# Mask triangles of the first layer moved to GpSimd, and small TensorE work in column strips

## The chip, the cores and the metric

The kernel runs on one core of a Trainium2 chip. The metric is device time in microseconds (us) from the first to the last instruction. Before the change the median of three runs is 2272.32 us (2268.7 to 2274.12). The profile is one execution of 2267.0 us.

A core has five engines with queues of their own that run in order: TensorE (PE, and PEld for its weight loads), VectorE (DVE), ScalarE (ACT), GpSimd (POOL) and SyncE (SP). They wait for each other through semaphores. GpSimd and SyncE also issue DMA transfers, in the order in which they stand in their queues.

## The reference: what is computed

Four attention layers follow one another, each of the form x + attention(layernorm(x)) on x of 2048 rows and 640 columns in bfloat16. Layers 0 and 2 (A) use a causal window of 256 keys; layers 1 and 3 (B) see all keys. All have 32 heads of 20 columns.

```python
mask = (idx[:, None] - idx[None, :] >= 0) & (idx[:, None] - idx[None, :] < W)   # W = 256, layers A
scores = jnp.where(mask[None, None], scores, -1e9)
p = _softmax(scores, axis=-1)
o = jnp.einsum("bhqk,bhkd->bhqd", p, v)
return (lambda x, *d: x.transpose(*d))(o, 0, 2, 1, 3).reshape(B, S, D) @ wo
...
x = x + _A_ref(_layernorm(x, axis=-1), A_wqkv, A_wo)
x = x + _B_ref(_layernorm(x, axis=-1), B_wqkv, B_wo)
```

The pair of lines at the end is run twice with the same weights.

## The kernel before

Work is cut into units: one layer, one chunk of 512 queries (four chunks, c), one group of four heads (eight groups, g). Layer 3's and layer 1's first chunks are cut further by keys. Within a unit the work goes by banks. A bank is a PSUM bank of 128 keys by 512 columns for one head: scores are computed with the keys on the partitions, so the probabilities can go straight into the product with the values. Two or three banks make a tile; the tiles alternate between two halves of the scores' PSUM.

For each tile the kernel emits, in this order: the score matmuls (line 1305, four heads in four row strips of the array), one exponential on ScalarE from PSUM to a bfloat16 tile pt in SBUF (line 1336), then side work, then the products of probabilities and values of a group of banks two or three tiles back (P·V, line 1369, in column strips of 21 columns), and last the masks of the tile before. In the windowed layers P·V trails by three tiles.

The values carry a column of ones, so row 20 of each head's strip in the output holds the sum of the probabilities. When a unit ends, VectorE copies the output to SBUF (line 856), and a tail (t_tail) is queued for every two units: it picks the row sums by small matmuls with a selector of four columns (line 1042), takes reciprocals on VectorE (line 1047), splits them into two bfloat16 halves, transposes them (line 1059), spreads them over the heads' rows by matmuls (line 1080) and multiplies (line 1084).

Side work is a list of Python generators (LayerNorm, projections, values, output projection, tails). A planner written into the kernel keeps a credit per tile and a due unit for each task, and so fixes the order of all instructions when the program is built. It also keeps an account of TensorE's activity and fills quiet places with matmuls whose result nobody reads (unread)[...]. Projections and fillers use by_columns (line 297): one product as four matmuls of 32 output columns each, in four column strips of the array. Weights of the projections are loaded by DMA from GpSimd's queue (line 334), and projected keys and queries are written to DRAM from the same queue (line 530).

LayerNorm's task (t_ln) scales 128 rows on VectorE (line 414), transposes them in five full 128 x 128 pieces on TensorE (line 432) and copies them out (line 320, on ScalarE or VectorE).

Masks. A windowed unit of a later chunk has three kinds of bank per head, m = 0, 1, 2, each with two key blocks laid into 512 columns. In blocks of 128 columns, m = 0 has triangles in blocks 0, 1 and 3, m = 1 in blocks 1 and 2, and m = 2 in blocks 0, 2 and 3: eight for each head. The unmasked blocks are full. In layer 0, line 1406 sets the two triangles of m = 1 with GpSimd's affine_select, in place on pt. Line 1416 multiplies all 512 columns (from the first block in use) of m = 0 and m = 2 by a bfloat16 mask on VectorE, one instruction for neighbouring banks of one m in a tile. Layer 2 does all masks on VectorE. In the first chunk the banks hold fewer blocks.

Layer 0 and the first part of layer 1 are woven: from the last group of layer 0's second chunk on, units of both alternate. Up to there, ScalarE copies the projections out of PSUM, after it VectorE does.

Of the kernel before, what the change touches and what calls it, by code (L numbers as in the profile page):

```python
# [12 lines left out]
ALU = mybir.AluOpType  # L13
ACT = mybir.ActivationFunctionType

P = 128
# [7 lines left out]
C = 512  # L24
# [22 lines left out]
def kernel(  # L47
# [10 lines left out]
    nc = tc.nc  # L58
# [33 lines left out]
    ident = big.tile([P, P], BF16, name="ident", tag="ident")  # L92
    nhalf = big.tile([P, 4], F32, name="nhalf", tag="nhalf")
    sel4 = big.tile([P, 4], BF16, name="sel4", tag="sel4")
    spread4 = big.tile([64, 4, P], BF16, name="spread4", tag="spread4")
    masks = big.tile([P, 3, C], BF16, name="masks", tag="masks")
# [8 lines left out]
    op = ps[:, 7, :]  # L105
# [10 lines left out]
    for h in range(2):  # L116
        for n in range(2):
            a = n * D + h * HD
# [10 lines left out]
    def load_wop(w, dense):  # L129
# [9 lines left out]
        out=ident[:], in_=ident[:], compare_op=ALU.not_equal, fill=1.0,  # L139
        base=0, pattern=[[-1, P]], channel_multiplier=1,  # L140
# [5 lines left out]
    for m, b, ge in (  # L146
# [4 lines left out]
        v = masks[:, m, b * P : (b + 1) * P]  # L151
        nc.gpsimd.affine_select(
            out=v, in_=v, compare_op=ALU.is_ge if ge else ALU.is_gt, fill=0.0,
            base=0, pattern=[[1 if ge else -1, P]], channel_multiplier=-1 if ge else 1,
# [138 lines left out]
    def by_columns(out_, lhsT, rhs, start, stop):  # L293

        for j in range(4):
            r = slice(32 * j, 32 * j + 32)
            nc.tensor.matmul(out_[r], lhsT=lhsT[:, r], rhs=rhs, start=start, stop=stop)  # L297
# [92 lines left out]
    def t_ln(l, c):  # L390
        while ("x", l, c) not in ready:
            yield ("wait", 1)
        yield from room("xnT", "ln")
        for n in (1, 0):
            order = worder[l, n]
            if order and not any(e in wtiles for e in order):
                wtiles[order[0]] = get_w(*order[0])
        users[l, c] = 9 if (l, c) == (0, 0) else (11, 12, 11, 11)[l]
        mv = mvs.pop((l, c))
        rstd = lnp.tile([P, 4], F32, name="rstd", tag="rstd")  # L400
        nc.gpsimd.tensor_scalar(  # L401
            out=rstd[:], in0=mv[:, :, 1], scalar1=EPS, scalar2=1.0, op0=ALU.add, op1=ALU.mult
        )
        nc.gpsimd.tensor_tensor(out=rstd[:], in0=rstd[:], in1=nhalf[:], op=ALU.pow)
        yield ("wait", 2)
        nmr = lnp.tile([P, 4], F32, name="nmr", tag="nmr")
        nc.vector.scalar_tensor_tensor(
            out=nmr[:], in0=mv[:, :, 0], scalar=-1.0, in1=rstd[:], op0=ALU.mult, op1=ALU.mult
        )
        xt = xtp.tile([P, KD, C], BF16, name="xnT", tag="xnT")  # L410

        def normed(i):
            xn = xnp.tile([P, D], BF16, name="xn", tag="xn")
            nc.vector.tensor_scalar(
                out=xn[:], in0=x_sb[:, 4 * c + i, :],
                scalar1=rstd[:, i : i + 1], scalar2=nmr[:, i : i + 1],
                op0=ALU.mult, op1=ALU.add,
            )
            return xn

        rows = deque([normed(0)])
        yield ("wait", 1)
        for i in range(4):
            if i < 3:
                rows.append(normed(i + 1))
            xn = rows.popleft()
            mb = yield from take_m()
            for _ in range(1+(l<2)):
                unread(mb)
            trp = ps[:, mb, :].bitcast(BF16)[:, 0 : KD * P].rearrange("p (c m) -> p c m", c=KD)  # L430
            for dc in range(KD):
                nc.tensor.transpose(  # L432
                    out=trp[:, dc, :], in_=xn[:, dc * P : (dc + 1) * P], identity=ident[:]
                )
            evac(xt[:, :, i * P : (i + 1) * P], trp)
            drop_m(mb)
            yield ("pe", 0.4)
        xnT[l, c] = xt
        live["ln"] -= 1
        ready.add(("xnT", l, c))  # L440
# [192 lines left out]
    def unread(b):  # L633

        by_columns(ps[:, b, :], ident, masks[:, 0, :], True, True)
        state["heat"] += 1.0
# [386 lines left out]
    def t_tail(us):  # L1023
        final = us[-1][0:3] == (3, NC - 1, G - 1)

        def fill(count):

            for n in range(count * final):
                nc.tensor.matmul(
                    ps[:, 0, :], lhsT=ident[:], rhs=masks[:, 0, :], start=True, stop=True  # L1030
                )

        n = len(us)
        yield ("wait", 2)
        fill(2)
        mb = yield from take_m()
        warm_bank(mb)
        zp = ps[:, mb, 0 : 16 * n]
        for i, (l, c, g, oT) in enumerate(us):
            for qb in range(4):  # L1040
                a = 16 * i + 4 * qb
                nc.tensor.matmul(  # L1042
                    zp[:, a : a + 4], lhsT=oT[:, qb * P : (qb + 1) * P],
                    rhs=sel4[:], start=True, stop=True,
                )
        rz = rzp.tile([P, 2, 16], F32, name="rz", tag="rz")[:, 0:n, :]
        nc.vector.reciprocal(out=rz.rearrange("p u r -> p (u r)"), in_=zp)
        drop_m(mb)

        hl = rzp.tile([P, 2, 2, 16], BF16, name="hl", tag="hl")[:, 0:n]  # L1050
        nc.vector.tensor_copy(out=hl[:, :, 0, :], in_=rz)
        nc.vector.tensor_tensor(out=hl[:, :, 1, :], in0=rz, in1=hl[:, :, 0, :], op=ALU.subtract)
        yield ("pe", 0.25)
        fill(3)
        yield ("wait", 2)
        mb = yield from take_m()
        warm_bank(mb)
        rp = ps[0 : 32 * n, mb, :].bitcast(BF16)[:, 0:P]
        nc.tensor.transpose(
            out=rp, in_=hl.rearrange("p u n r -> p (u n r)"), identity=ident[:]  # L1060
        )
        rT = rzp.tile([64, P], BF16, name="rT", tag="rT")
        nc.vector.tensor_copy(out=rT[0 : 32 * n], in_=rp)
        drop_m(mb)
        yield ("pe", 0.1)
        fill(1)
        yield ("wait", 2 if state["tick"] < last_tick[0] else 1)
        for i in range(n):
            yield from scaled(*us[i], 32 * i, rT, fill)
        if any(packed(l, c) for l, c, g, oT in us):  # L1070
            yield ("wait", 2)
        for u in us:
            yield from settle(*u)
# [121 lines left out]
    with tc.manual_schedule():  # L1195
# [14 lines left out]
        n = 0  # L1210
        last_layer = sum(len(u.banks) for u in units[: index[3, 1, 0, None]])
        placed = {}
        while n < last_layer:
            size = 2 if len(tiles) % 2 and narrow(banks[n][0]) else 3
            u = banks[n][0]
# [52 lines left out]
        while ended is None or t < ended + 8:  # L1268
# [3 lines left out]
            if t < len(tiles) or banks:  # L1272
# [9 lines left out]
                for b in cur:  # L1282
                    u = b[0]
# [18 lines left out]
                for n in range(2):  # L1302
                    for i, (u, j, m, b0, subs, first, last, end) in enumerate(cur):
                        for kc, q0, qn, col in subs[n : n + 1]:
                            nc.tensor.matmul(  # L1305
                                sp[:, i, col * P : (col + qn) * P],
                                lhsT=u.k(kc, j), rhs=u.q(j, q0, qn), start=True, stop=True,
# [22 lines left out]
                i = 0  # L1330
                while i < n_b:
                    b0 = cur[i][3]
                    k = i
                    while k < n_b and cur[k][3] == b0:
                        k += 1
                    nc.scalar.activation(  # L1336
                        out=pt[:, i:k, b0 * P :], in_=sp[:, i:k, b0 * P :],
                        func=ACT.Exp, scale=SCALE,
                    )
                    i = k  # L1340
# [5 lines left out]
                r = rate(t)  # L1346
# [6 lines left out]
            for n in range(2 if n_b == 0 or t > closed + 1 else 0):  # L1353
                u = pts[0][3][0] if pts else None
# [11 lines left out]
                for m, (kc, q0, qn, col) in enumerate(subs):  # L1366
                    for _, pg, i, b in group:
                        j = b[1]
                        nc.tensor.matmul(  # L1369
                            op[32 * j : 32 * j + VW, q0 * P : (q0 + qn) * P],  # L1370
                            lhsT=u.v(kc, j), rhs=pg[:, i, col * P : (col + qn) * P],
                            start=(first and m == 0), stop=(last and m == len(subs) - 1),
                            skip_group_check=u.windowed,
                        )
                if end and u.aside:
                    pair = side_done(u)
                    for n, j in enumerate(u.aside):
                        nc.tensor.matmul(  # L1378
                            op[32 * j : 32 * j + VW, :], lhsT=u.v(NT - 1, j),
                            rhs=pair[n // 2][:, n % 2, :], start=False, stop=True,  # L1380
# [12 lines left out]
            if t > 0 and masked is not None:  # L1393
                cur_, pt_ = masked
                i = 0
                while i < len(cur_):
                    m, b0 = cur_[i][2:4]
                    k = i
                    while k < len(cur_) and cur_[k][2] == m:
                        k += 1  # L1400
                    if m == 1 and cur_[0][0].l == 0:
                        for b in (1, 2):
                            if b < b0:
                                continue
                            v = pt_[:, i:k, b * P : (b + 1) * P]
                            nc.gpsimd.affine_select(  # L1406
                                out=v, in_=v, compare_op=ALU.is_gt if b == 1 else ALU.is_ge, fill=0.0,
                                base=0, pattern=[[0, k - i], [-1 if b == 1 else 1, P]],
                                channel_multiplier=1 if b == 1 else -1,
                            )  # L1410
                    elif m is not None:
                        cols = slice(max(b0, m == 1) * P, 3 * P if m == 1 else C)
                        mv_ = masks[:, m, cols].unsqueeze(1).to_broadcast(
                            (P, k - i, cols.stop - cols.start)
                        )
                        nc.vector.tensor_tensor(  # L1416
                            out=pt_[:, i:k, cols], in0=pt_[:, i:k, cols], in1=mv_, op=ALU.mult
                        )
                    i = k
# [36 lines left out]
```

The softmax here doesn't subtract the row's maximum and nothing guards it: scores larger than these inputs give would overflow.

## Time and profile before

| What | Value |
|---|---|
| median of three runs | 2272.32 us |
| lowest, highest | 2268.7, 2274.12 us |
| profiled execution, first to last instruction | 2267.0 us |
| ScalarE busy | 2166.5 us (96%) |
| TensorE busy, by its modelled ends | 1973.3 us (87%) |
| VectorE busy | 1269.8 us (56%) |
| GpSimd busy | 326.2 us (14%) |
| GpSimd's selects, line 1406 | 126, 55.8 us, between 21 and 383 us |
| VectorE's mask multiplies, line 1416 | 331, 191.0 us, of which 136 and 86.0 us between 20 and 385 us |
| full-array transposes, line 432 | 300 matmuls, 28.4 us |
| row sums, line 1042 | 512 matmuls, 22.7 us |
| transposes of reciprocals, line 1059 | 65 matmuls, 15.8 us |

A busy time is the union of an engine's instructions. A group's row gives the line, the engine, the operation, what is written and read with its shape, the number of instructions, the busy time, the mean length of one in ns, and the idle time of the engine just before them with what ended it. A shape such as 128*32 128x512 of a matmul means 128 rows and 32 columns of the array, moving 512 columns; 32*128 is a row strip and 128*32 a column strip. The chain of work is followed back from the last instruction, at each step to what released it.

### The profile page before, as it was taken

How to read it: one execution, taken by the hardware profiler on the slowest of the kernel's cores; microseconds unless marked ns; L12 is line 12 of the kernel's file. 1: busy time of each engine (PE TensorE's matmuls, PEld its weight loads, DVE VectorE, ACT ScalarE, POOL GpSimd, SP SyncE). 2: the span in 40 equal slices, each digit the busy share in tenths (PEclk: the TensorE clock that was granted, in tenths of full speed). 3: DMA queues.
4: the chain of work that ended last, by engine and by line, in shares of the span. 5: the costliest groups of instructions: out<-in, count | busy, mean ns of one | idle time of the engine just before them, and what ended most of it. 6: DMA issues, size and time to landing. Idle time of an engine off the chain costs nothing.

```text
span 2267.0 us, 65801 instructions
## 1 busy us (share of the span) xinstructions
PE 1973.3 (87%) x28523; PEld 776.0 (34%) x28524; DVE 1269.8 (56%) x2158; ACT 2166.5 (96%) x1740; POOL 326.2 (14%) x571
## 2 busy tenths in 40 slices
PE   8999998988888888888888988898888888888887
PEld 3444343334333333333333443342322222222222
DVE  6766575435554565555564644442566666656665
ACT  7789899999999989999899999999999999999998
POOL 4454334201100122001210022002000000000000
PEclk9999999999999999999999999999999999999999
DMA  6233223422210233002330033103211111111100
GB/s 195 72 91 94 74 87 93 100 76 50 78 34 15 60 88 104 17 28 58 93 90 15 16 106 105 31 17 91 65 51 31 31 40 34 31 31 43 42 21 16
DMA packets 88384, 136.80 MB, mean 60 GB/s; under 512 B 20766, under 2 KB 63486, under 8 KB 88094
## 3 DMA queue, kind: packets, MB, share of 16 engines
q1 hardware_dynamic: 68878, 79.43, 12.6%
q0 software_dynamic: 19216, 53.17, 8.0%
q8 instruction: 223, 3.65, 0.7%
q14 instruction: 67, 0.55, 0.1%
HBM read 99.52 MB, written 27.79 MB: 56 GB/s over the span
## 4 chain that ended last, share of the span: by engine, by line
ACT 49%; PE 23%; issue 17%; DVE 9%; POOL 1%; DMA 1%; SPq 0%; ACTq 0%; DVEq 0%; POOLq 0%
ACT pt L1336 47%; PE ps L297 14%; PE ps L1305 5%; PE ps L1369 2%; DVE pt L1416 1%; ACT ka L1336 1%; DVE x_sb L562 1%; DVE st L320 1%; DVE on L1084 1%; PE ps L432 1%; PE ps L1080 0%; DVE vs L320 0%; DVE va L320 0%; PE ps L1042 0%; DVE raw_o L909 0%
## 5 line engine op out<-in xcount | busy, mean ns | idle before, releaser
L1336 ACT ACTIVATE pt<-ps 128x1536 bf16<-128x1536 f32 (+2 forms) x1636 | 2089.3, 1462 | 64.8 <-PE ps L1305 56.2
L297 PE MATMUL ps<-masks,ident 128*32 128x512 bf16 x6452 | 553.2, 388 | 113.2 <-ACT pt L1336 59.1
L1305 PE MATMUL ps<-qt,kt 32*128 32x512 bf16 x4004 | 545.7, 384 | 85.5 <-ACT pt L1336 77.6
L1369 PE MATMUL ps<-pt,vt 128*21 128x512 bf16 x3844 | 392.2, 382 | 0.1
L1305 PEld LDWEIGHTS <-kt 32*128 32x128 bf16 x4004 | 163.4, 91 | 544.1 <-issue 526.8
L297 PEld LDWEIGHTS <-ident 128*32 128x32 bf16 x6452 | 162.0, 94 | 361.6 <-issue 350.4
L1416 DVE TENSOR_TENSOR pt<-pt,masks 128x1024 bf16<-128x1024 bf16 (+6 forms) x331 | 191.0, 604 | 154.9 <-ACT pt L1336 154.1
L297 PE MATMUL ps<-xnT,wqk 128*32 128x512 bf16 x3320 | 221.7, 385 | 17.1 <-DVE st L320 7.9
L320 DVE CAST st<-ps 128x512 bf16<-128x512 f32 x134 | 92.6, 691 | 188.1 <-PE ps L297 187.7
L909 DVE TENSOR_SCALAR xnT<-ps 128x512 int32<-128x512 f32 x92 | 63.6, 691 | 191.4 <-PE ps L902 191.3
L297 PE MATMUL ps<-wop,on 128*32 128x320 bf16 x3712 | 156.9, 301 | 13.3 <-DVE x_sb L562 8.4
L1305 PE MATMUL ps<-qa,ka 32*128 32x384 bf16 (+2 forms) x1408 | 117.9, 276 | 32.0 <-ACT pt L1336 29.4
L1369 PEld LDWEIGHTS <-vt 128*21 128x21 bf16 x3956 | 102.5, 91 | 110.4 <-issue 64.8
L1084 DVE TENSOR_TENSOR on<-on,ps 128x512 bf16<-128x512 bf16 x128 | 86.3, 683 | 67.0 <-PE ps L1080 65.3
L297 PE MATMUL ps<-wv,xnT 128*32 128x320 bf16 x2560 | 112.4, 301 | 10.8 <-DVE on L1084 3.3
L297 PEld LDWEIGHTS <-wqk 128*32 128x32 bf16 x3320 | 79.1, 96 | 112.8 <-issue 59.4
L562 DVE TENSOR_TENSOR x_sb<-x_sb,ps 128x320 bf16<-128x320 bf16 x120 | 58.0, 483 | 104.9 <-PE ps L297 104.7
L297 PEld LDWEIGHTS <-on 128*32 128x32 bf16 x3712 | 92.8, 96 | 65.9 <-issue 49.2
L856 DVE CAST on<-ps 128x512 bf16<-128x512 f32 x112 | 77.0, 687 | 59.9 <-PE ps L1378 32.9
L401 POOL TENSOR_SCALAR rstd<-mv 128x4 f32<-128x4 f32 x15 | 3.8, 253 | 712.4 <-DVE mv L388 702.8
L1305 PEld LDWEIGHTS <-ka 32*128 32x128 bf16 x1408 | 43.2, 92 | 117.0 <-issue 110.9
L1369 PE MATMUL ps<-pt,va 128*21 128x384 bf16 (+2 forms) x1408 | 76.9, 281 | 4.6 <-POOL pt L1406 3.5
(100 smaller groups left out, 1589.8 us busy)
## 6 DMA issues: line engine op xcount, KB each, us to landing
vt<-v_d SPq DMA_DIRECT2D x48, 336.0 KB
kt<-k_d SPq DMA_DIRECT2D x192, 80.0 KB
wqk<-in_B_wqkv_dram POOLq DMA_DIRECT2D x80, 160.0 KB, 3.6
wqk<-in_A_wqkv_dram POOLq DMA_DIRECT2D x70, 160.0 KB, 3.3
k_d<-st POOLq DMA_DIRECT2D x75, 128.0 KB, 2.2
q_d<-st POOLq DMA_DIRECT2D x75, 128.0 KB, 2.2
qt<-q_d SPq DMA_DIRECT2D x384, 20.0 KB
v_d<-vs POOLq DMA_DIRECT2D x16, 336.0 KB, 3.4
```

The costliest lines, as they stand in the source:

```text
L297: nc.tensor.matmul(out_[r], lhsT=lhsT[:, r], rhs=rhs, start=start, stop=stop)
L320: nc.vector.tensor_copy(out=out_, in_=in_)
L401: nc.gpsimd.tensor_scalar(out=rstd[:], in0=mv[:, :, 1], scalar1=EPS, scalar2=1.0, op0=ALU.add, op1=ALU.mult)
L432: nc.tensor.transpose(out=trp[:, dc, :], in_=xn[:, dc * P : (dc + 1) * P], identity=ident[:])
L562: nc.vector.tensor_tensor(out=xv, in0=had, in1=yp, op=ALU.add)
L856: nc.vector.tensor_copy(out=oT, in_=op)
L909: V.tensor_scalar(out=xi.bitcast(I32)[:, i * C : (i + 1) * C], in0=side["psum"], scalar1=SCALE * LOG2E * E23, scalar2=-128.0 * E23, op0=AL ...
L1084: nc.vector.tensor_tensor(out=oT, in0=oT, in1=zb, op=ALU.mult)
L1305: nc.tensor.matmul(sp[:, i, col * P : (col + qn) * P], lhsT=u.k(kc, j), rhs=u.q(j, q0, qn), start=True, stop=True,)
L1336: nc.scalar.activation(out=pt[:, i:k, b0 * P :], in_=sp[:, i:k, b0 * P :], func=ACT.Exp, scale=SCALE,)
L1369: nc.tensor.matmul(op[32 * j : 32 * j + VW, q0 * P : (q0 + qn) * P], lhsT=u.v(kc, j), rhs=pg[:, i, col * P : (col + qn) * P], start=(first ...
L1416: nc.vector.tensor_tensor(out=pt_[:, i:k, cols], in0=pt_[:, i:k, cols], in1=mv_, op=ALU.mult)
```

## The change

The masks of layer 0 are split differently. GpSimd now also sets the triangle in block 3 of m = 0 and that in block 0 of m = 2, so it has four of the eight. VectorE multiplies only columns 0 to 255 of m = 0 and columns 256 to 511 of m = 2, where the other two triangles of each bank lie. Each such group of banks has one instruction on either engine where there was one on VectorE. Layer 2 stays as it was. The aim is to relieve VectorE in the first layer.

The transposes of LayerNorm, the row sums and the transposes of the reciprocals are emitted in column strips of 32 columns, as the projections already are: 20 matmuls in place of 5, 32 in place of 8 for two units, and two in place of one. The aim is to keep TensorE in one tile shape. The planner's accounts are not touched, so the order of the tasks stays the same.

```diff
--- before.py
+++ after.py
@@ -429,9 +429,12 @@
                 unread(mb)
             trp = ps[:, mb, :].bitcast(BF16)[:, 0 : KD * P].rearrange("p (c m) -> p c m", c=KD)
             for dc in range(KD):
-                nc.tensor.transpose(
-                    out=trp[:, dc, :], in_=xn[:, dc * P : (dc + 1) * P], identity=ident[:]
-                )
+                for j in range(4):
+                    a = dc * P + 32 * j
+                    nc.tensor.transpose(
+                        out=trp[32 * j : 32 * j + 32, dc, :], in_=xn[:, a : a + 32],
+                        identity=ident[:],
+                    )
             evac(xt[:, :, i * P : (i + 1) * P], trp)
             drop_m(mb)
             yield ("pe", 0.4)
@@ -1039,10 +1042,7 @@
         for i, (l, c, g, oT) in enumerate(us):
             for qb in range(4):
                 a = 16 * i + 4 * qb
-                nc.tensor.matmul(
-                    zp[:, a : a + 4], lhsT=oT[:, qb * P : (qb + 1) * P],
-                    rhs=sel4[:], start=True, stop=True,
-                )
+                by_columns(zp[:, a : a + 4], oT[:, qb * P : (qb + 1) * P], sel4[:], True, True)
         rz = rzp.tile([P, 2, 16], F32, name="rz", tag="rz")[:, 0:n, :]
         nc.vector.reciprocal(out=rz.rearrange("p u r -> p (u r)"), in_=zp)
         drop_m(mb)
@@ -1056,9 +1056,11 @@
         mb = yield from take_m()
         warm_bank(mb)
         rp = ps[0 : 32 * n, mb, :].bitcast(BF16)[:, 0:P]
-        nc.tensor.transpose(
-            out=rp, in_=hl.rearrange("p u n r -> p (u n r)"), identity=ident[:]
-        )
+        for i in range(n):
+            nc.tensor.transpose(
+                out=rp[32 * i : 32 * i + 32], in_=hl[:, i].rearrange("p n r -> p (n r)"),
+                identity=ident[:],
+            )
         rT = rzp.tile([64, P], BF16, name="rT", tag="rT")
         nc.vector.tensor_copy(out=rT[0 : 32 * n], in_=rp)
         drop_m(mb)
@@ -1398,17 +1400,26 @@
                     k = i
                     while k < len(cur_) and cur_[k][2] == m:
                         k += 1
-                    if m == 1 and cur_[0][0].l == 0:
-                        for b in (1, 2):
-                            if b < b0:
-                                continue
-                            v = pt_[:, i:k, b * P : (b + 1) * P]
-                            nc.gpsimd.affine_select(
-                                out=v, in_=v, compare_op=ALU.is_gt if b == 1 else ALU.is_ge, fill=0.0,
-                                base=0, pattern=[[0, k - i], [-1 if b == 1 else 1, P]],
-                                channel_multiplier=1 if b == 1 else -1,
-                            )
-                    elif m is not None:
+                    split = m is not None and cur_[0][0].l == 0
+                    for b in ((3,), (1, 2), (0,))[m] if split else ():
+                        if b < b0:
+                            continue
+                        later = (m, b) in ((1, 1), (0, 3))
+                        v = pt_[:, i:k, b * P : (b + 1) * P]
+                        nc.gpsimd.affine_select(
+                            out=v, in_=v, compare_op=ALU.is_gt if later else ALU.is_ge, fill=0.0,
+                            base=0, pattern=[[0, k - i], [-1 if later else 1, P]],
+                            channel_multiplier=1 if later else -1,
+                        )
+                    if split and m != 1:
+                        cols = slice(max(b0, 0) * P, 2 * P) if m == 0 else slice(2 * P, C)
+                        mv_ = masks[:, m, cols].unsqueeze(1).to_broadcast(
+                            (P, k - i, cols.stop - cols.start)
+                        )
+                        nc.vector.tensor_tensor(
+                            out=pt_[:, i:k, cols], in0=pt_[:, i:k, cols], in1=mv_, op=ALU.mult
+                        )
+                    elif m is not None and not split:
                         cols = slice(max(b0, m == 1) * P, 3 * P if m == 1 else C)
                         mv_ = masks[:, m, cols].unsqueeze(1).to_broadcast(
                             (P, k - i, cols.stop - cols.start)
```

## The prediction

> **What bounds the kernel now.** First the whole-span busy line of the page (PE 87%, ACT 96%, DVE 56%, POOL 14%), which averages over unlike stages. Then busy time by stretch, cut at the ends of what the change touches: line 1406 (the GpSimd selects) runs from 21 to 383 us and nowhere else, and the last LayerNorm transpose starts at 1518.5 us.
>
> ```profile
> core 0: us, PE busy (x) PEld busy (x) DVE busy (x) ACT busy (x) POOL busy (x), PEclk, DMA share, GB/s
> 20.00:180.00 160.00, 145.44 (x2612) 69.74 (x2600) 104.87 (x230) 133.39 (x175) 78.28 (x149) 0.97 0.35 100
> 180.00:385.00 205.00, 188.58 (x3217) 83.65 (x3213) 135.41 (x266) 187.45 (x162) 87.35 (x153) 0.98 0.30 86
> 385.00:1520.00 1135.00, 991.47 (x14605) 408.62 (x14602) 586.93 (x1066) 1102.38 (x856) 136.66 (x213) 1.00 0.22 59
> 1520.00:2267.00 747.00, 632.46 (x7944) 206.97 (x7937) 429.42 (x560) 733.05 (x537) 14.02 (x20) 0.99 0.14 40
> ```
>
> After 385 us ScalarE's exponentials fill 97% and then 98% of the time: 33 + 14 us of idleness are all that anything can win there. Layer one (365 us) is another regime: ScalarE idles 27 + 18 us, and no engine is full. The chain of work that ended last, taken from 20 to 385 us, says which one sets the pace.
>
> ```profile
> by line: PE ps L297 32.4%; ACT pt L1336 17.9%; PE ps L1305 12.0%; issue 7.4%; PE ps L1369 6.1%; DVE pt L1416 4.0%; DVE on L1084 2.1%; PE ps L432 2.1%; POOL pt L1406 1.6%; DVE stats L386 1.1%; DMA wqk<-in_A_wqkv_dram 1.0%; DVE stats L387 1.0
> ```
>
> TensorE holds more than half of it. Of what is edited, VectorE's mask has 14.8 us (4.0%), GpSimd's select 6.0 us. The groups by shape in the same stretch give the prices of the masks, and the waits show how little GpSimd's lateness costs today.
>
> ```profile
> L1416 DVE TENSOR_TENSOR pt<-pt,masks 128x1024 bf16<-128x1024 bf16 x58 | 40.5, 705 | 6.1 <-ACT pt L1336 6.1
> L1416 DVE TENSOR_TENSOR pt<-pt,masks 128x1536 bf16<-128x1536 bf16 x21 | 20.3, 968 | 2.0 <-ACT pt L1336 1.8
> L1416 DVE TENSOR_TENSOR pt<-pt,masks 128x512 bf16<-128x512 bf16 x41 | 17.9, 439 | 5.6 <-ACT pt L1336 5.5
> L1406 POOL TENSOR_SCALAR_AFFINE_SELECT pt<-pt 128x256 bf16<-128x256 bf16 x52 | 23.7, 477 | 36.5 <-ACT pt L1336 35.9 <-POOL pt L1406 0.3
> ```
>
> ```profile
> PE ps L1369 <- POOL pt L1406: 3.5, 3, 1.9
> ```
>
> The first fence reads busy us, mean ns | idle before; the second, from the table of waits, total us, times, longest.
>
> [...] From the starts of successive matmuls, less the columns streamed at 2.4 per ns, a matmul in another mode than its forerunner starts 0.09 to 0.12 us late (medians: column strips to full array 109 ns, full array to column strips 96, row strips to column strips 102, 64 columns to column strips 120); within a mode the figure is 3 ns. [...] the row sums here, four columns wide, start 25 ns apart, which is 60 columns.
>
> [...] a select of 384 takes 524 ns alone and 800 to 990 ns when a mask multiply started first, and it then ends 0.38 us after the multiply (0.27 us for 256, 0.15 us for 128 elements).
>
> **Part one, transposes and row sums in strips.** Removed are the switches into and out of full-array (or 64-column) mode. Counting in TensorE's order the mode on both sides of every group of lines 432, 1042 and 1059: two switches go where both neighbours are column strips, one where one is a row-strip score matmul. That is 39 switches from 20 to 180 us, 32 to 385 us, 179 to 1520 us, 61 after: 311 of 0.1 us, 31 us of TensorE. Added are instructions: 5 transposes become 20 in each of 60 sets, 8 row sums become 32, one transpose becomes two. The lower bound of their cost is nothing: windowed P·V in strips of 128 columns shows four matmuls 56 ns after the four before (259.758 to 259.814 us), the pace of full transposes. The upper bound is the densest issue in the trace, 16 instructions in 123 ns: the 64 loads and matmuls of one row sum would take 0.49 us instead of 0.20, 0.3 us for each of 65. I take zero, since strips start 3 to 4 ns apart when queued, and keep 0.3.
>
> On the path: in layer one a wait of ScalarE of over 60 ns (between the group and the exponential of the next scores) follows 28 of the 54 groups, and TensorE has over half the chain; half of 71 x 0.1 us is 3.5 us gained. From 385 to 1520 us such a wait follows 10 of 102 groups, after that none, so about 2 of 24 us come through; the exponentials hide the rest. Gain: 5.5 us.
>
> **Part two, VectorE's half.** In layer one a bank's 512 masked columns become 256. With the trace's undisturbed medians (128 elements 215 ns, 256 283, 384 349, 512 416, 768 549), 58 x (705-416) + 21 x (968-549) + 41 x (439-283) + 9 x (545-283) of 768 elements + 3 x (748-349) of 1152 + 4 x (404-215) of 384 = 36 us less of 86 us: VectorE goes from 240 to 204 us of 365. What it frees is seen in who is queued behind a mask: PSUM drains and line 1084, on which TensorE waited 7.9 us in ten places. Of the 14.8 us of masks on the chain 42% would be 6 us[...]. I take 3.5 us, bounds 0 and 8.
>
> **Part three, GpSimd's half.** Each of the 136 multiplies gets a companion select on the same tile, woken by the same exponential: 67 of 256 (404 ns), 24 of 384 (524), 45 of 128 (284): 52 us alone. In the pairs on record that start within 0.15 us VectorE nearly always goes first, [...] up to 41 us more. GpSimd goes from 166 us of 365 to between 218 and 259 us.
>
> The finished tile comes no sooner: multiply of 768 then select, 0.55 + 0.38 us, against 0.95 us for the whole multiply before. It may come later, since the select now stands in GpSimd's queue between the weight loads (0.87 us each) and the k/q stores (0.57 us). Waiting behind it are P·V matmuls three tiles later, and the next weight loads. One place in the timeline (here the rows of GpSimd and TensorE alone) shows what a crowded GpSimd does already:
>
> ```profile
> 274.64 1.39 POOL L1406 TENSOR_SCALAR_AFFINE_SELECT pt<-pt 128x256 bf16<-128x256 bf16 x2
> ...
> 275.99 1.13 POOL L530 DMA_DIRECT2D k_d<-st  x2
> ...
> 277.11 1.73 POOL L334 DMA_DIRECT2D wqk<-in_A_wqkv_dram  x2
> ...
> 280.79 1.26 PE L297 MATMUL ps<-xnT,wqk 128*32 128x512 bf16 x20 [1.18 <-DMA wqk<-in_A_wqkv_dram]
> ```
>
> [...] TensorE loses 1.18 us. Of the weight loads from 114 to 178 us and from 346 to 376 us, thirteen land only 0.6 to 2.9 us before their first matmul. I take the select waits of P·V to grow from 3.5 to 6 us and two more places like this one: a cost of 4 us, bounds 0 and 15.
>
> **The sum.** -5.5 - 3.5 + 4 = -5 us: 2272.3 becomes 2267 us.
>
> **Rivals.** (a) Both halves pay: GpSimd's queue absorbs the selects, as its 6 to 10 us pauses near 74 and 103 us suggest, and a lighter VectorE shortens every drain: -5.5 - 8 = -13.5, 2259 us. Against it: GpSimd's pauses lie where no weight loads are. (b) GpSimd becomes the limit of layer one, slower than before: from 77.8 to 87.9 us it is busy 8.7 of 10.1 us, and the five multiplies of that stretch bring five selects, 2 us more. Cost 15, gain of VectorE 1, of the strips 5.5 less 1 for issue: +9.5, 2282 us. Against it: so far P·V waited for a select three times. (c) All is hidden, and ScalarE's pace after 385 us takes back what layer one wins: 2272 us. Against it: ScalarE and layer two's loads follow layer one's end directly.
>
> **How the numbers follow.** Forecast 0.45, (a) 0.20, (b) 0.26, (c) 0.09. The limit of 0.2% is 4.5 us, and the forecast's -5 lies beside it, so a little over half of it counts as faster, the rest as the same. Faster 0.20 + 0.24 = 0.44; same 0.20 + 0.09 + 0.03 of the milder (b) = 0.32; slower 0.24. The range takes in (a) with a little room, 2257, and (b), 2282; the clock grants (four stretches at half clock, 3.4 to 6.8 us long, lie in layer one) can shift either end by 2 us.
>
> **What would show it.** Right: the transposes' group shows 128*32 x1200, row sums x2048, no gap of 0.1 us around them; the multiplies' busy time in layer one near 50 us; selects x262, many near 0.7 us; ScalarE's idle time from 20 to 385 us falls from 45 to about 40 us; beyond 385 us nothing moves by more than 2 us. Wrong toward (b): P·V's wait for the selects or the wait for wqk grows by 5 us or more, GpSimd over 70% busy. Wrong in part one: row sums that take 0.5 us or more. Wrong in part two: multiplies that stay near their old lengths[...].

## The result and the profile after

The changed kernel takes 2257.95 us in the median of four runs (2255.1 to 2260.86), against 2273.11 us before in the runs beside them: ratio 0.9937, 95% interval 0.9916 to 0.9958. A second series of the same kernel (e12 below) gives 2258.45 us and 0.9941 (0.9927 to 0.9955). The change is 0.6% faster, some 14 us, where the forecast said 5. The direction and the range held; the size is that of rival (a).

"Layer one" below is what the prediction calls so: the stretch up to some 385 us, in which layer 0 is woven with the first parts of layer 1.

Busy time by stretch of the kernel after, for the same stretches as before:

```profile
core 0: us, PE busy (x) PEld busy (x) DVE busy (x) ACT busy (x) POOL busy (x), PEclk, DMA share, GB/s
20.00:180.00 160.00, 146.81 (x3071) 72.59 (x3067) 94.90 (x236) 136.53 (x177) 108.38 (x233) 0.97 0.36 103
180.00:385.00 205.00, 187.88 (x3615) 84.75 (x3603) 123.72 (x266) 191.19 (x166) 102.10 (x201) 0.98 0.30 86
385.00:1520.00 1135.00, 980.00 (x16006) 411.79 (x16009) 588.80 (x1068) 1102.10 (x856) 136.34 (x212) 1.00 0.22 59
```

From 20 to 385 us VectorE is busy 219 us in place of 240, GpSimd 210 in place of 166 (below the forecast's bounds of 218 to 259), and ScalarE gets 7 us more done. In the third row ScalarE is as before (1102.1 us beside 1102.4): the win is made in layer one. A finer ruler shows it. The 1740 instructions of ScalarE come in the same order in both kernels, so the n-th can be set beside the n-th. The last exponential of layer one (number 346) ends at 383.3 us before and 374.5 us after; number 420 is 9.6 us earlier, number 680 still 9.6, the last one 10.0. In between the lead wanders from 7.4 to 12.0 us; it isn't taken back, so rival (c) falls. (Of the lead, 1.0 us is there at 20 us already, when hardly anything edited has run; by the last instruction of all these two traces lie 8.6 us apart, less than the 14 us of the medians.)

The chain of work from 20 to 385 us, after:

```profile
by line: PE ps L297 37.2%; PE ps L1307 14.4%; ACT pt L1338 14.0%; issue 6.8%; PE ps L1371 6.4%; DVE on L1086 2.2%; POOL pt L1409 2.0%; PE ps L434 1.4%; DVE pt L1419 1.4%; ACT xnT L318 1.2%; DMA wqk<-in_A_wqkv_dram 1.0%; POOL wqk L334 0.9%; 
```

VectorE's mask (now line 1419) falls from 4.0% to 1.4% of the chain, with 0.4% more on line 1427, where tiles that begin with a bank of layer 1 still get the full multiply; GpSimd's select rises only from 1.6% to 2.0%. Groups by shape and, from the table of waits, the only wait of P·V for a select:

```profile
L1409 POOL TENSOR_SCALAR_AFFINE_SELECT pt<-pt 128x256 bf16<-128x256 bf16 x116 | 50.6, 450 | 38.2 <-ACT pt L1338 36.8 <-issue 1.1
L1419 DVE TENSOR_TENSOR pt<-pt,masks 128x512 bf16<-128x512 bf16 x55 | 25.6, 470 | 7.4 <-ACT pt L1338 6.6 <-POOL pt L1409 0.7
L1419 DVE TENSOR_TENSOR pt<-pt,masks 128x256 bf16<-128x256 bf16 x44 | 14.7, 343 | 5.9 <-ACT pt L1338 5.9
L1419 DVE TENSOR_TENSOR pt<-pt,masks 128x768 bf16<-128x768 bf16 x21 | 12.6, 601 | 2.4 <-ACT pt L1338 2.3
```

```profile
PE ps L1371 <- POOL pt L1409: 2.3, 2, 1.7
```

P·V waits less for the selects, although there are twice as many: 2.3 us in place of 3.5. The multiplies take about 55 us in place of 86, each 50 to 60 ns over its quiet length (416, 283 and 549 ns). In e3 below, without the new selects, the first two groups are back at 434 and 284 ns.

### The profile page after: what moved, and what is told of

It reads as the page before. It is cut to its first block, busy times and chain, and to the rows that moved or that the text cites. A ratio compares the mean times of both kernels' runs of the same rounds, so it can differ in the third digit from the quotient of the medians.

```text
span 2258.4 us, 71013 instructions
## 1 busy us (share of the span) xinstructions
PE 1950.3 (86%) x31022; PEld 777.9 (34%) x31023; DVE 1246.0 (55%) x2158; ACT 2164.1 (96%) x1740; POOL 371.5 (16%) x701
## 4 chain that ended last, share of the span: by engine, by line
ACT 50%; PE 22%; issue 17%; DVE 9%; POOL 1%; DMA 1%; SPq 0%; ACTq 0%; DVEq 0%; POOLq 0%
ACT pt L1338 48%; PE ps L297 14%; PE ps L1307 5%; PE ps L1371 2%; ACT ka L1338 1%; DVE st L320 1%; DVE on L1086 1%; DVE pt L1427 1%; DVE x_sb L565 1%; PE ps L1082 1%; DVE va L320 1%; DVE vs L320 0%; PE ps L434 0%; DVE xnT L320 0%; POOL pt L1409 0%
## 5 line engine op out<-in xcount | busy, mean ns | idle before, releaser
L1427 DVE TENSOR_TENSOR pt<-pt,masks 128x512 bf16<-128x512 bf16 (+7 forms) x201 | 108.2, 571 | 138.2 <-ACT pt L1338 137.6
L297 PEld LDWEIGHTS <-on 128*32 128x32 bf16 x5760 | 117.3, 95 | 75.7 <-issue 53.6
L1409 POOL TENSOR_SCALAR_AFFINE_SELECT pt<-pt 128x256 bf16<-128x256 bf16 (+2 forms) x256 | 103.4, 427 | 70.7 <-ACT pt L1338 64.6
```

Source lines behind the costliest of these rows:

```text
L1409: nc.gpsimd.affine_select(out=v, in_=v, compare_op=ALU.is_gt if later else ALU.is_ge, fill=0.0, base=0, pattern=[[0, k - i], [-1 if later ...
L1427: nc.vector.tensor_tensor(out=pt_[:, i:k, cols], in0=pt_[:, i:k, cols], in1=mv_, op=ALU.mult)
```

## The experiments

**A second ruler.** The times of one kernel spread over 10 us and more, and the spread goes with something that the profile shows. In the clock record of every trace TensorE runs at full or at half clock, for 3.4 or 6.8 us at a time in those of before and after. From a run's mean granted clock follows its time at half clock, 2 x (1 - clock) x time. Over 107 runs of the kernel before the time is 2259 us plus 0.32 us for each us at half clock (correlation 0.90); over ten runs of the kernel after, 2250 us plus 0.30. The table takes 0.33 for all, and its last column (median less 0.33 x half clock) compares the kernels at full clock. It is an estimate from this fit; the fits of all thirteen kernels run from 0.30 to 0.46. The kernel before was run again beside each series, on three chips, with medians of 2273.4 (e1 to e4), 2272.2 (e5 to e8) and 2270.1 us (e9 to e12); the ratios compare within a series.

| Kernel | runs | median us | ratio to before (95%) | us at half clock | at full clock |
|---|---|---|---|---|---|
| before | 107 | 2272.2 | | 40.9 | 2258.7 |
| changed (with e12) | 10 | 2258.5 | 0.9937, 0.9941 | 27.1 | 2249.6 |
| e1 strips alone | 6 | 2264.9 | 0.9961 (0.9946-0.9976) | 40.8 | 2251.4 |
| e2 masks alone | 21 | 2265.6 | 0.9978 (0.9967-0.9990) | 36.2 | 2253.7 |
| e3 no new selects | 5 | 2250.8 | 0.9899 (0.9884-0.9915) | 13.5 | 2246.3 |
| e4 selects on top | 6 | 2288.2 | 1.0066 (1.0045-1.0088) | 54.9 | 2270.1 |
| e5 before, more filler | 22 | 2266.2 | 0.9983 (0.9972-0.9994) | 20.4 | 2259.5 |
| e6 changed, more filler | 6 | 2259.8 | 0.9949 (0.9929-0.9969) | 27.1 | 2250.9 |
| e7 weights from SyncE | 22 | 2266.7 | 0.9980 (0.9971-0.9989) | 36.3 | 2254.7 |
| e8 six selects | 18 | 2264.9 | 0.9969 (0.9958-0.9980) | 34.0 | 2253.7 |
| e9 LayerNorm strips | 14 | 2263.6 | 0.9969 (0.9957-0.9980) | 29.4 | 2253.9 |
| e10 row-sum strips | 13 | 2268.2 | 0.9984 (0.9975-0.9993) | 31.8 | 2257.7 |
| e11 three selects | 6 | 2256.0 | 0.9936 (0.9920-0.9951) | 20.3 | 2249.3 |

**e1, strips alone.** The mask lines of before, the three strip edits of the change.

> The strips alone, masks as before. The forecast's term: 5.5 us faster than before (about 2267.5 us), 3.5 us of it won by the end of layer one. Rival 1 (the strips carry nearly the whole gain): 12 us or more faster (2261 us). Rival 2 (the masks carry it): 5 us or less.

Measured: 2264.9 us, 7 to 9 us faster by median and ratio. Between the forecast's 5.5 and rival 1's 12; the median time at half clock hardly changes, so over these six runs the win looks like TensorE's work itself (e9 below says otherwise). The strips are about half of the whole. The trace can't show where: it is of the slowest of the six runs, with 27 us at half clock in layer one beside 20 in that of before, and leads by 2.1 us there.

**e2, masks alone.** The three strip edits undone.

> The masks alone, TensorE as before. The forecast's terms (-3.5 for VectorE, +4 for GpSimd): no change, 2273 us. Rival 1 (the strips carry the gain): within 2 us of before. Rival 2 (a lighter VectorE pays and GpSimd costs nothing): 8 us faster, 2265 us, all of it won before the end of layer one.

Measured: 2265.6 us, 5 to 8 us faster by ratio and median. The forecast of no change is wrong and rival 2 nearly right in size; in the trace the lead is 4.7 us at the end of layer one.

**e3, without GpSimd's new half.**

```diff
-                    for b in ((3,), (1, 2), (0,))[m] if split else ():
+                    for b in ((), (1, 2), ())[m] if split else ():
```

> The changed kernel without GpSimd's two new triangles (layer one's masks of block 3 of m = 0 and block 0 of m = 2 are left out, so keys outside the window count there). VectorE's multiplies stay short. The forecast's term for GpSimd: 4 us faster than the changed kernel, about 2254 us. Rival 2 (GpSimd's queue absorbs the selects): the same as the changed kernel, 2258 us.

Measured: 2250.8 us, 7.7 us below the changed kernel (9 by the ratios). So the selects do cost, about twice the 4 us of the forecast. Against e1, which differs only in the width of VectorE's multiplies, it is 14 us faster: this is VectorE's relief, where the forecast had 3.5 us and a bound of 8. The multiplies of e3, for the lengths above:

```profile
L1419 DVE TENSOR_TENSOR pt<-pt,masks 128x512 bf16<-128x512 bf16 x55 | 23.6, 434 | 7.3 <-ACT pt L1338 7.3
L1419 DVE TENSOR_TENSOR pt<-pt,masks 128x256 bf16<-128x256 bf16 x44 | 12.1, 284 | 5.9 <-ACT pt L1338 5.9
```

The chunk change near 90 us shows the clock at work. The stretch from 84 to 104 us of e1, of the changed kernel and of e3:

```profile
84.00:104.00 20.00, 17.37 (x298) 7.41 (x293) 15.12 (x38) 14.80 (x15) 7.82 (x18) 0.66 0.19 53
```

```profile
84.00:104.00 20.00, 17.61 (x372) 8.95 (x374) 15.73 (x42) 16.16 (x15) 12.11 (x29) 0.83 0.15 41
```

```profile
84.00:104.00 20.00, 16.13 (x396) 8.73 (x392) 16.05 (x44) 16.55 (x16) 8.20 (x19) 1.00 0.17 47
```

The granted clock (third number from the end) is 0.66, 0.83 and 1.00, and TensorE completes 298, 372 and 396 matmuls in the same 20 us. Over layer one the traces have 27, 17 and 3 us at half clock, and from its first exponential to its last it takes 365.9, 359.1 and 353.0 us, while TensorE's idle time hardly differs (33, 29 and 29 us). These are single executions, and that of e1 is its slowest run, so they show the link and not its size.

**e4, selects without relief.**

```diff
-                        cols = slice(max(b0, 0) * P, 2 * P) if m == 0 else slice(2 * P, C)
+                        cols = slice(max(b0, 0) * P, C)
```

> The changed kernel with VectorE multiplying all 512 columns as before, GpSimd's four triangles besides (the values are the same, two triangles are masked twice). It has GpSimd's cost without VectorE's relief. The forecast's terms: 3.5 us slower than the changed kernel, 2261.5 us. Rival 2: 8 us slower, 2266 us. Rival 1: within 2 us of it.

Measured: 2288.2 us, 30 us slower than the changed kernel and slower than before. It does not answer its question, because it adds a wait: the full multiply touches the columns that the select has just written, and waits for it. Its groups in layer one, with the idle time ahead of them and what ended it:

```profile
L1419 DVE TENSOR_TENSOR pt<-pt,masks 128x1024 bf16<-128x1024 bf16 x49 | 36.0, 739 | 21.0 <-POOL pt L1409 20.8
L1419 DVE TENSOR_TENSOR pt<-pt,masks 128x512 bf16<-128x512 bf16 x34 | 17.9, 528 | 10.8 <-POOL pt L1409 10.8
```

It shows something else: when VectorE is held up some 46 us by GpSimd, TensorE waits 14.8 us for line 1086 alone, layer one spends 51 us at half clock and takes 391 us (in a trace of the slowest of its six runs). That the change gives the two engines separate columns is a part of why it works.

**e5 and e6, more filler.** If the clock is a cause and does not only go along, then filler matmuls that leave less time at half clock must by themselves help the kernel before.

```diff
-                state["least"] = (1.76 if state["unit"] >= woven else 1.0) * n_b / 3
+                state["least"] = 1.76 * n_b / 3
```

> The kernel before, with more of the planner's unread matmuls in the first 17 units (floor of TensorE's activity account 1.76 for each three banks there, as later, in place of 1.0). Clock theory (in the runs so far each us at half clock costs some 0.36 us of time, and part of the gain is a clock that stays open): the 43 us at half clock fall by 15 or more and the time by 4 to 6 us, to about 2268. Rival (the half clock only accompanies stalls that have other causes, and fillers just stand in the way): no faster than before, or slower.

> The changed kernel with the same additional unread matmuls. Clock theory: its 27 us at half clock fall to 15 or less, and the time by some 4 us, to about 2254; the gain of the change on top of fillers shrinks from 15 to about 12 us. Rival: the same as the changed kernel or slower.

Measured: on the kernel before, the half clock falls from 41 to 20 us and the time by 6 us to 2266.2, while the time at full clock stays where it was (2259.5 beside 2258.7). The traces show what the edit amounts to. The instructions of VectorE, ScalarE and GpSimd are the same in number and order; TensorE has 21 matmuls more, all unread: 20 among the others between 90 and 96 us, at the chunk change, and one at the end. From 88 to 126 us, before and e5:

```profile
88.00:126.00 38.00, 34.36 (x630) 17.03 (x629) 29.98 (x72) 28.43 (x29) 13.89 (x30) 0.87 0.15 44
```

```profile
88.00:126.00 38.00, 32.82 (x674) 17.41 (x670) 31.30 (x74) 29.95 (x30) 15.63 (x34) 1.00 0.19 51
```

The two stretches at half clock of before (6.8 us at 91 us and 3.4 us at 119 us) are absent, and ScalarE gains 2.0 us on before between 92 and 124 us. So the clock is a cause: nothing was relieved, and 21 useless matmuls save 6 us in the median. How far is less sure. The trace is of one of e5's slowest runs (2275.6 us); elsewhere it has stretches at half clock that before lacks, the first of them at 50 us, where it falls back by 1.7 us, and its layer one is no shorter. Ten of the 20 us are seen to go at this place; where the others went one trace can't tell. On the changed kernel it is inconclusive: 2259.8 us, from 2250 to 2263, with the same 27 us in the median; its one trace has 7 instead of 17 us at half clock in layer one, which is 2 us shorter, and the rest lies in later layers, which the edit does not reach.

**e7, weights from SyncE's queue.**

```diff
-            nc.gpsimd.dma_start(out=t[:], in_=wq_view[l % 2][:, :, a : a + P])
+            if l < 2:
+                nc.sync.dma_start(out=t[:], in_=wq_view[l % 2][:, :, a : a + P])
+            else:
+                nc.gpsimd.dma_start(out=t[:], in_=wq_view[l % 2][:, :, a : a + P])
```

> The changed kernel with the projection weights of layers one and two loaded from SyncE's queue in place of GpSimd's, so that no select stands ahead of a weight load and no load ahead of a select. Leaving out the new selects saved 7 us. If these 7 us are the queue (loads and selects behind each other), 4 to 7 us faster than the changed kernel, about 2252 us. [...]

Measured: 2266.7 us, 8 us slower than the changed kernel. P·V no longer waits for a select at all, so little was to be had there; but the weights now stand behind SyncE's loads and come late:

```profile
PE ps L297 <- DMA wqk<-in_B_wqkv_dram: 6.2, 2, 4.0
PE ps L297 <- DVE on L1089: 5.5, 9, 1.7
...
PE ps L297 <- DMA wqk<-in_A_wqkv_dram: 2.9, 2, 1.5
```

The new queue's 9 us of waiting hide what the old one cost, so the queue's share in the 7.7 us of e3 stays open. What multiplies and selects cost each other shows in lengths: against their undisturbed medians VectorE's multiplies are stretched by some 7 us in the changed kernel and by 2 us in e3, and the selects by 11 and 5 us.

**e8 and e11, the dose.** Six triangles on GpSimd with VectorE multiplying 128 columns, and three with m = 2 back on VectorE in full.

```diff
-                    for b in ((3,), (1, 2), (0,))[m] if split else ():
+                    for b in ((1, 3), (1, 2), (0, 2))[m] if split else ():    # e8
+                    for b in ((3,), (1, 2), ())[m] if split else ():          # e11
```

> The changed kernel with six of the eight triangles on GpSimd and VectorE multiplying 128 columns for each bank. If VectorE's load is what matters, 3 us faster than the changed kernel, 2255 us. If GpSimd is at its limit (rival b of the forecast, one step later), 7 us slower or more, 2265 us.

> The changed kernel with three of the eight triangles on GpSimd: the bank m = 2 goes back to VectorE with all 512 columns. With two on GpSimd (strips alone) 2265 us were measured, with four 2258, with six 2265. If VectorE's relief and GpSimd's crowding both grow evenly, between two and four, 2261 us. Rival (GpSimd's cost comes late, above four): no gap to two selects' VectorE cost, also about 2261; if GpSimd's cost is felt from the first select on, 2258 us or less.

Measured: 2264.9 and 2256.0 us. With the strips in place, two, three, four and six triangles on GpSimd give 2265, 2256, 2258.5 and 2265 us; three and four differ by less than their intervals. With six, VectorE is hardly lighter (210 us busy from 20 to 385 us beside 219), GpSimd is busy 250 us, and the waits of rival (b) are there:

```profile
PE ps L1371 <- POOL pt L1409: 5.7, 7, 1.9
ACT pt L1338 <- POOL pt L1409: 4.1, 3, 2.3
```

Three is as good as four and is not shown to be better.

**e9 and e10, which strips.** LayerNorm's transposes alone; the row sums and the reciprocals' transposes alone.

> Of the strips, LayerNorm's transposes alone (masks and row sums as before). By the count of mode switches they hold 42 of the 71 removed in layer one and 63 of the 179 from there to 1520 us: if the strips' 8 us are switches in layer one, about 5 us faster than before, 2268 us. Rival (the row sums carry it): 2 us or less.

> Of the strips, the row sums and the transposes of the reciprocals alone. 29 of the 71 switches in layer one, 116 of the 179 after it, 61 of 61 at the end: if only layer one counts, 3 us faster than before, 2270 us. Rival (switches after layer one count as well): 6 us or more, 2267 us.

Measured: 2263.6 and 2268.2 us beside 2270.1 us for the kernel before in the same series, 7 and 2 to 4 us by median and ratio. LayerNorm's transposes carry the larger part of the strips' gain, as the count for layer one had it. Not all of it is switches: e9 spends 29 us at half clock beside 36 for before in its own series, and at 0.33 each this is 2 of its 7 us. The 177 switches that the row sums and reciprocals lose after layer one give little.

**e12, the changed kernel once more.**

> The changed kernel once more, to have it beside the others on one chip: 2258 us, its time following 0.35 us for each us at half clock, with some 27 us at half clock.

Measured: 2258.45 us with 27.1 us at half clock in the median, as expected.

## Why the prediction was right, and where its sum was not

The forecast was faster by 5 us; 14 us came, inside the range. That the direction came right is in part luck: the forecast's masks were a net loss of half a us (-3.5 + 4), and only its strips made it faster; the masks alone (e2) gain 5 to 8 us. Rival (a) has the size, 13.5 us, but not the mechanism: the selects are not absorbed (they cost 7.7 us by e3), and VectorE's relief comes to 14 us where it had 8. Step by step:

**Switches of mode: right in count and price.** TensorE's order holds 3670 changes of mode before and 3362 after, 308 fewer (311 counted). Less the columns streamed (512 in 216 ns in a queue of full-array matmuls, 2.4 per ns), 92 to 120 ns lay between one of these groups and the next column-strip matmul, and nothing is left (medians from -49 to 7 ns). The strips cost what the lower bound said: first to last start is 235 ns for 20 transposes (234 for five) and 216 ns for 32 row sums (189 for eight). Here is a row sum between row-strip scores and a column-strip projection, after:

```profile
243.87 0.39 PE L1307 MATMUL ps<-qt,kt 32*128 32x512 bf16 x2
244.18 0.36 PE L297 MATMUL ps<-sel,on 128*32 128x4 bf16 x32
244.40 0.62 PE L297 MATMUL ps<-xnT,wqk 128*32 128x512 bf16 x8
```

"Half of 71 x 0.1 us is 3.5 us gained" was too cautious: the strips gain 7 to 9 us, as much as all 71 switches of layer one at 0.1 us. That these are what was won isn't shown: LayerNorm's 42 switches alone go with 7 us (e9), in part through the clock. A reason that is argued and not isolated: transposes of LayerNorm wait for VectorE's rows and copies (6.1 and 1.7 us from 20 to 385 us before) and are waited for by the copies (8.9 us on VectorE, 2.5 on ScalarE), so a delay is handed on.

**VectorE's half: the length right, its worth not.** The multiplies fell by some 31 us (36 forecast): they are stretched by 7 us, and nine of the 136 lie in tiles that begin with a bank of layer 1 and stay as they were, without a companion select (256 selects in all, 262 forecast). "I take 3.5 us, bounds 0 and 8": with e3 against e1, 14 us, beyond the bound. At full clock the estimate is 5 us, inside it.

**GpSimd's half: the cost came, its steps did not.** "The select waits of P·V to grow from 3.5 to 6 us" failed: they shrank to 2.3 us. "VectorE nearly always goes first" was misread: among the multiplies and selects that start within 0.15 us of each other, VectorE is first in 9 and GpSimd in 14 in the trace of before, and in 25 and 27 after. The "up to 41 us more" did not come: the selects' stretch stayed at 11 us in all. Still the selects cost 7.7 us by e3, of which some 3 us at full clock, where the forecast had 4. Which wait carries them is open: ScalarE waits 2.9 us for a select in two places, where before has none, but e1, with two triangles, has 2.6 us of this too.

**The failing step is the clock.** "The clock grants (four stretches at half clock, 3.4 to 6.8 us long, lie in layer one) can shift either end by 2 us." It was put in as noise of the range, and is a term of the sum: the median time at half clock falls from 40.9 to 27.1 us. Added up:

| Term | forecast | at full clock | with the clock |
|---|---|---|---|
| strips (e1 - before) | -5.5 | -7.3 | -7.3 |
| VectorE's half (e3 - e1) | -3.5 | -5.1 | -14.1 |
| GpSimd's half (changed - e3) | +4 | +3.3 | +7.7 |
| sum | -5 | -9.1 | -13.7 |

In this order the middle column is near the forecast in each term. The rest, 4.6 us, is 13.8 us less at half clock at 0.33 each. To which edit it belongs is not settled: here it all sits in the masks, but with the masks taken first (e2, then the strips) the masks gain 6.6 us, 5.0 of them at full clock, and the strips 7.1 us, 4.1 of them at full clock. The middle column is thus sure to some 3 us a term. e5 shows that time at half clock is a cause of time; that less of it comes with a lighter VectorE and more again with a crowded GpSimd is read from 41, 13.5 and 27 us in e1, e3 and the changed kernel, and from e4's 55. What brings on a stretch at half clock was not isolated, and e3 and e1 have only five and six runs. The full-clock column rests on the fit: with 0.40 in place of 0.33 VectorE's half is -3.2 and the sum -8.2.

**What was foretold to stay.** After layer one the lead moves between 7.4 and 12.0 us, at times 3 us from the 8.8 of layer one's end where 2 were foretold, and ends at 10.0; ScalarE's idle time from 20 to 385 us falls from 44 to 37 us (45 to 40 foretold).

## What to carry to other kernels

Price a relief of a feeding engine twice: once by what waits for it, and once by what it does to TensorE's time at half clock (40.8 us in e1, 13.5 in e3); by the fit the second was the larger here, 9.0 us beside 5.1. A few unread matmuls where the clock falls are a cheap test of it (21 in e5, for 6 us). Small full-array matmuls in a stream of column strips cost two switches here, of 109 and 96 ns in the median, for a handful of columns, and in strips they cost next to nothing more (1 ns for five transposes, 27 ns for eight row sums). When two engines share the masking of one tile, give them separate columns (in e4, where they overlap, VectorE waits some 46 us), and look for the best dose by trying one step either side: here three or four of eight.

## What the runs showed of the hardware

- A us at half clock costs about a third of a us in this kernel: fits of 0.30 to 0.46 over thirteen kernels. It costs where ScalarE is 97% busy too: across the stretch of 3.4 us at 839 us in the trace of before, which that of after lacks, the lead goes from 10.1 to 11.5 us.
- With twenty unread matmuls more between 90 and 96 us (e5) the clock granted from 88 to 126 us is 1.00 in place of 0.87, and ScalarE gains 2.0 us between 92 and 124 us.
- Thirty-two matmuls of four columns in four column strips start within 216 ns, eight in the full array within 189 ns: 7 ns from one to the next in place of 27, on average.
- Selects of 128, 256 and 384 elements take 284, 404 and 524 ns undisturbed; with 256 of them in place of 126, they are stretched by 11 us in all, as before.
